# Moving the load and conversion of half of w_in from the attention stretch into the experts' stretch

## The chip, the cores and the metric

The kernel runs on one core of one Trainium2 chip. Times are device microseconds (us) of one launch. Several runs are made of each kernel, and the median is compared. One more execution is recorded by the hardware profiler; it has its own time and its own span, from its first to its last instruction.

## The reference

```
x = attention(q_l, k_l, v_l, q_g, k_g, v_g)        # 4 batches, 8 heads, 512 local + 32 global tokens, head size 64,
                                                   # local window of 32 on both sides; softmax
x = x as [2176 tokens, 512]
logits = x @ phi                                   # 512 x 32: 8 experts of 4 slots
d = softmax of logits over the tokens; slot_input = d.T @ x
for e in 8 experts: slot_out[e] = relu(slot_input[e] @ w1[e]) @ w2[e]      # w1[e] 512 x 1024, w2[e] 1024 x 512
c = softmax of logits over the slots; x = c @ slot_out
out = (relu(x @ w_in) ** 2) @ w_out                # w_in 512 x 2048, w_out 2048 x 512
```

w_in and w_out arrive as 8-byte floats; everything else is 4-byte. The kernel makes 4-byte floats of w_in and w_out itself, with integer operations.

## The kernel before, in words

The program has three stretches, and each engine runs its instructions in the order in which the code issues them.

**Attention** (0 to 182 us in the profile) is a loop over 44 units (a block of 32 queries, local or global, half of the heads). At step n of the loop (line 708) the scores of unit n are made (`emit_S`, line 314), the exponentials of unit n-1 (`emit_exp`), the transposes of unit n-2 (`emit_T`), and the products with V of two older units together (`emit_AV`, line 367; `av_at`, line 633, says at which step). V lies in a ring of three blocks (`load_v`, line 165). The block for the next pair of units can be loaded only when the products of the present pair have read the oldest block, so `load_v(s + 3)` is issued behind them (line 682), and the next products wait for it. K and Q blocks are loaded the same way, with four transfers each. All loads of this stretch, but for the first four, are issued by SyncE (SP), whose one queue the 16 DMA engines serve; a load that has to wait on SP holds up all that are behind it.

**Weights of the experts.** w1 and w2 are 64 pieces of 512 KB, loaded in the order of the list `order` (line 567) by `load_piece` (line 573). A piece needs a room, a granule of 1,024 floats on each of 128 partitions, in arena A, B or T; `room` (line 126) lists the free ones. Attention begins with 23 free rooms. The tuple `PIECES` (line 309) says how many pieces are asked for at each of the 44 steps; an ask without a room does nothing. 20 more rooms come free inside and at the end of attention (`free`, line 595: each room given is used at once), so 43 pieces are on their way when attention ends. The other 21 wait until the experts' multiplies have used up a piece and `done` (line 811) gives its room back.

**The first half of w_in** (8 chunks of 512 KB) is loaded and converted within attention. `win_load` (line 558) puts a chunk into the buffer `cv_raw` and is issued at steps 3, 7, 12, 16, 21, 25, 30 and 34; `win_convert` (line 562) gives five parts, placed on later steps by `CONV` and `CONV_AT` (line 299): `split` and mostly `rest` on ScalarE (ACT), `clamp`, `shift` and half of `join` on VectorE (DVE), the last addition on GpSimd (POOL). The result goes to `win_sb`, four granules of A that hold nothing else. `cv_raw` and the two scratch halves `cv_y` and `cv_r` take two granules of B until steps 38 and 39.

**Experts** (182 to 221 us). `layer1(gr, c0, c1)` multiplies the slots of four experts with w1 (line 902), `layer2` with w2 (line 929); the calls are in lines 956 to 989. A piece of w2 holds 128 rows of two experts, in runs of 2 KB. A room that comes free is asked for the next load at once (`fill`). Near the end of the list stands the first chunk of w_out ("raw"); 15 more chunks of w_out and the second half of w_in follow in the last stretch. After `layer2_T(1)` (line 989), `G_direct` (line 1029) multiplies the experts' output with `win_sb`.

**The final network** (221 us to the end) is bound by its multiplies (lines 1107 to 1109).

Of the kernel before, what the change touches and what calls it, by code (L numbers as in the profile page):

```python
# [10 lines left out]
I32 = mybir.dt.int32  # L11
# [13 lines left out]
def local_global_attention__soft_moe__relu2_kernel(  # L25
# [15 lines left out]
    nc = tc.nc  # L41
# [66 lines left out]
    q_buf = Bq.carve(H, 2 * D)  # L108
    cv_raw = Bq.carve(DM, 2).bitcast(I32)
    cv_y, cv_r = Bq.carve(DM), Bq.carve(DM).bitcast(I32)  # L110
    kT = Bq.carve(HP, B, 8, QB)
# [13 lines left out]
    tri = pe_buf[2][:, 0, 0:2 * QB].rearrange("p (n q) -> p n q", n=2)  # L125
    room = {"a": A.granules(7, 23), "b": Bq.granules(15, 22), "t": []}

# [141 lines left out]
    for s in range(NJ):  # L269
# [28 lines left out]

    CONV = (4, 9, 13, 18, 22, 27, 31, 36)
    CONV_AT = (  # L300
        (0, 0, 1, 2, 3), (-1, 1, 1, 2, 3), (0, 0, 1, 2, 3), (0, 0, 0, 2, 3), (0, 1, 1, 2, 3), (0, 0, 0, 2, 3),
        (0, 1, 2, 2, 3), (0, 0, 1, 1, 2),
    )
    REST_ON_ACT = (0, 0, 1, 0, 1, 1, 1, 1)

    MOE_D = (3, 4, 5)
    MOE_AT = ((0, 2, 2), (0, 1, 0), (0, 1, 2))

    PIECES = (
        0, 0, 0, 0, 1, 2, 0, 0, 1, 1, 1, 1, 0, 1, 1, 2, 0, 1, 1, 2, 0, 0, 0, 1, 1, 1, 1, 0, 1, 2, 1, 3, 0, 1,  # L310
        0, 1, 0, 0, 0, 0, 2, 2, 1, 1,
    )
# [244 lines left out]

    def win_load(n):
        c, f = divmod(n, WRES)
        convert_load(cv_raw, w_in[128 * c:128 * c + 128, 2 * CW * f:2 * CW * f + 2 * CW])  # L560

    def win_convert(n):
        c, f = divmod(n, WRES)
        return convert(cv_raw, win_sb[:, c, CW * f:CW * f + CW].bitcast(I32), cv_y, cv_r, REST_ON_ACT[n], nc.gpsimd)


    order = [(1, 4 * g + j, c) for g in range(2) for c in range(NC) for j in range(4)]
    order += [(2, 4 * g + j, c) for g in range(2) for c in range(8) for j in range(0, 4, 2)]
    order.insert(62, ("raw", 0, 0))
    piece, raws = {}, {}  # L570
    nxt = [0]

    def load_piece():
        if nxt[0] == len(order):
            return False
        kind, e, c = order[nxt[0]]
        if kind == "raw":
            if not room["a"]:
                return False
            nxt[0] += 1  # L580
            return raw_load()
        at = next((r for r in ("tba" if kind == 2 and e >= 4 else "tab") if room[r]), None)
        if at is None:
            return False
        v = g = room[at].pop(0)
        nxt[0] += 1
        if kind == 1:
            nc.sync.dma_start(out=v, in_=w1[e, 128 * c:128 * c + 128, :])
        else:
            v = v.rearrange("p (e f) -> p e f", e=2)  # L590
            nc.sync.dma_start(out=v, in_=w2[e:e + 2, 128 * c:128 * c + 128, :].rearrange("e p f -> p e f"))
        piece[kind, e, c] = (v, at, g)
        return True
# [11 lines left out]
    with tc.manual_schedule():  # L605
# [46 lines left out]
        for i in range(NM - 1):  # L652
            l1 = ("l", NT * i + NT - 1, 1)
            d = av_at(index[l1]) - index[l1]
            for fns, pos, dd in zip(((moe_logits,), (moe_TT, moe_c_exp), (moe_S,)), MOE_AT[i], MOE_D):
                for fn in fns:
                    at(l1, pos, fn, i, d=d + dd)
        for n in range(NC * WRES):
            split, clamp, shift, rest, join = win_convert(n)
            u = units[CONV[n]]  # L660
            for f, pos, d in zip((split, rest, clamp, shift, join), (2, 2, 2, 2, 0), CONV_AT[n]):
                at(u, pos, f, d=d)
            if n + 1 < NC * WRES:
                after(u, win_load, n + 1, d=CONV_AT[n][-1])
        for n in range(2):
            after(u, free, "b", 2 + n, 3 + n, d=CONV_AT[-1][-1] + n)
        after(("l", 12, 0), free, "b", 0, 1)
# [37 lines left out]
        load_vg()  # L705
        late.setdefault(3, []).append((win_load, (0,)))
        late.setdefault(5, []).insert(0, (load_phi, ()))
# [101 lines left out]
        ps_h = ctx.enter_context(tc.tile_pool(name="ps_h", bufs=2, space=PSUM))  # L809

        def done(kind, e, c):
            _, at, g = piece.pop((kind, e, c))
            room[at].append(g)


# [113 lines left out]
        def layer2(gr, c0, c1):  # L929
            for c in range(c0, c1):  # L930
                for n in range(2):
                    if c == 0:
                        hps[2 + gr, n] = ps_o.tile([128, 256], F32, tag="o", name="ops")
                    for j in range(4):
                        e = 4 * gr + j
                        nc.tensor.matmul(hps[2 + gr, n][32 * j:32 * j + 32], hT[gr][:, 16 * c + SE * j:16 * c + SE * j + 32],
                                         piece[2, e - e % 2, c][0][:, e % 2, 256 * n:256 * n + 256], start=(c == 0),
                                         stop=(c == 7))
                for j in range(0, 4, 2):
                    done(2, 4 * gr + j, c)  # L940
                fill()
                if gr and c == 6:
# [33 lines left out]
        layer2_T(0)  # L976
        assert nxt[0] == len(order)
        yro = [room["a"].pop(0) for _ in range(3)]
# [199 lines left out]
```

## Time and profile before

| | |
|---|---|
| median of 3 runs (lowest to highest) | 445.91 us (445.83 to 448.59) |
| the profiled execution's own time | 447.44 us |
| its span | 444.7 us |
| mean granted clock of TensorE | 0.983 |
| busy: PE / DVE / ACT / POOL | 403.9 / 295.9 / 230.8 / 130.4 us |
| bytes moved by DMA | 68.94 MB |

How to read it: PE is TensorE, SP the queue on which SyncE issues loads. "Idle before" is the time in which an engine did nothing ahead of an instruction, and behind the arrow stands what ended it. The granted clock is a share of 2.4 GHz; 0.50 is 1.2 GHz. A PE that is called busy may be working at the lower clock. L167 is line 167: V loads; L525: chunks of w_in and w_out; L588 and L591: pieces of w1 and w2.

### The profile page before, as it was taken

The numbers are of one execution on the slowest core, as the hardware profiler recorded it, in microseconds if no ns is written. First come the engines' busy times: TensorE is split into PE (matmuls) and PEld (weight loads), VectorE is DVE, ScalarE is ACT, GpSimd is POOL, SyncE is SP. The second block draws the span as 40 slices with busy tenths as digits, with TensorE's granted clock in tenths as the row PEclk, the third lists the DMA queues.
The fourth block names the chain that finished last, engine by engine and source line by source line (L and its number), as shares of the span: only waits on it lengthen the run. The fifth ranks groups of instructions, "written<-read, shape, count | busy, mean of one in ns | idle before, by whom it ended". The sixth has DMA issues, their size and how long they took to land.

```text
span 444.7 us, 11332 instructions
## 1 busy us (share of the span) xinstructions
PE 403.9 (91%) x4387; PEld 310.4 (70%) x4387; DVE 295.9 (67%) x956; ACT 230.8 (52%) x535; POOL 130.4 (29%) x161
## 2 busy tenths in 40 slices
PE   7898789688789868999799999999999999999996
PEld 6677667576568655346368878787887888788885
DVE  5588756476787957521289999886998454744443
ACT  3678656588456423131257666566666444344442
POOL 6234424254245423120045542224554000000000
PEclk9999989899998989999999999999999999999999
DMA  8999999789995688899963333410000300300003
GB/s 153 193 256 208 246 248 238 190 187 243 229 211 145 180 253 286 307 377 387 400 235 96 109 127 96 141 50 0 0 2 7 136 0 1 143 1 1 0 0 118
DMA packets 58212, 68.94 MB, mean 155 GB/s; under 512 B 23216, under 2 KB 39600, under 8 KB 58160
## 3 DMA queue, kind: packets, MB, share of 16 engines
q1 hardware_dynamic: 55920, 65.61, 54.2%
q10 hardware_dynamic: 2240, 2.62, 1.9%
q8 instruction: 34, 0.56, 0.5%
q14 instruction: 18, 0.15, 0.1%
HBM read 63.77 MB, written 4.46 MB: 153 GB/s over the span
## 4 chain that ended last, share of the span: by engine, by line
PE 51%; DMA 23%; DVE 14%; issue 5%; ACT 4%; SPq 1%; POOL 1%; ACTq 0%; POOLq 0%; DVEq 0%
DMA arena_b<-in_v_l_dram 13%; PE ops L1107 9%; PE ops L1108 9%; PE ops L1109 9%; PE xp L383 4%; PE sp L326 4%; PE hps L909 3%; DMA arena_a<-in_moe_w_out_dram 3%; DMA arena_b<-in_moe_w_in_dram 3%; DMA arena_b<-in_moe_w_dram 3%; DVE arena_a L535 3%; PE hp L1073 2%; DVE al L1084 2%; DVE arena_a L548 2%; PE pp L364 2%
## 5 line engine op out<-in xcount | busy, mean ns | idle before, releaser
L1107 PE MATMUL ops<-w_hl,ah 128*128 128x512 f32 x272 | 107.6, 396 | 0.0
L1108 PE MATMUL ops<-w_hl,ah 128*128 128x512 f32 x272 | 106.7, 392 | 0.4 <-POOL w_hl L851 0.4
L1109 PE MATMUL ops<-w_hl,al 128*128 128x512 f32 x272 | 106.2, 390 | 0.0
L1077 DVE TENSOR_TENSOR arena_a<-hp,arena_a 128x384 f32<-128x384 f32 x96 | 46.8, 528 | 46.8 <-ACT arena_a L1076 46.6
L1076 ACT ACTIVATE arena_a<-hp 128x384 f32<-128x384 f32 x96 | 40.2, 471 | 68.6 <-PE hp L1073 63.4
L1109 PEld LDWEIGHTS ops<-w_hl,al 128*128 128x128 f32 x272 | 51.1, 188 | 11.6 <-DVE al L1084 0.6
L1107 PEld LDWEIGHTS ops<-w_hl,ah 128*128 128x128 f32 x272 | 51.0, 188 | 11.0 <-issue 0.8
L1108 PEld LDWEIGHTS ops<-w_hl,ah 128*128 128x128 f32 x272 | 51.1, 188 | 10.5 <-POOL w_hl L851 1.8
L1083 ACT ACTIVATE ah<-arena_a 128x384 fp32r<-128x384 f32 x96 | 45.0, 505 | 24.9 <-DVE arena_a L1077 24.9
L1084 DVE TENSOR_TENSOR al<-arena_a,ah 128x384 fp32r<-128x384 f32 x96 | 49.9, 560 | 8.2 <-ACT ah L1083 4.2
L347 POOL TENSOR_TENSOR arena_r<-arena_r,nm 128x512 f32<-128x512 f32 x32 | 35.7, 1115 | 65.9 <-DVE nm L334 47.6
L139 ACT ACTIVATE arena_b<-tp 64x256 f32<-64x256 f32 (+2 forms) x131 | 42.5, 348 | 16.5 <-PE tp L216 11.4
L383 PE MATMUL xp<-arena_b,arena_t 128*32 128x65 f32 x1408 | 26.7, 224 | 20.7 <-DMA arena_b<-in_v_l_dram 17.6
L550 POOL TENSOR_TENSOR arena_a<-arena_a 128x512 int32<-128x512 int32 x23 | 29.8, 1295 | 50.7 <-DVE arena_a L548 48.2
L383 PEld LDWEIGHTS xp<-arena_b,arena_t 128*32 128x32 f32 x1408 | 22.2, 111 | 26.3 <-issue 10.0
L326 PE MATMUL sp<-arena_b 128*64 128x128 f32 x512 | 38.5, 297 | 1.5 <-ACT arena_b L139 1.5
L334 DVE CUSTOM_DVE_ANT_0 arena_r<-sp,arena_r 128x128 f32<-128x128 f32 x128 | 29.5, 286 | 14.8 <-PE sp L326 14.0
L326 PEld LDWEIGHTS sp<-arena_b 128*64 128x64 f32 x512 | 30.2, 147 | 11.2 <-issue 8.8
L356 ACT ACTIVATE arena_r<-arena_r 128x512 f32<-128x512 f32 x44 | 27.6, 627 | 11.0 <-POOL arena_r L347 10.7
L364 PE MATMUL pp<-ident,arena_r 128*128 128x128 f32 x176 | 30.2, 297 | 2.8 <-ACT arena_r L356 2.8
L851 POOL TENSOR_TENSOR w_hl<-arena_a,w_hl 128x512 fp32r<-128x512 f32 x16 | 21.4, 1336 | 33.5 <-DMA arena_a<-in_moe_w_out_dram 17.6
L364 PEld LDWEIGHTS pp<-ident,arena_r 128*128 128x128 f32 x176 | 19.5, 145 | 9.5 <-ACT arena_r L356 3.7
(181 smaller groups left out, 574.0 us busy)
## 6 DMA issues: line engine op xcount, KB each, us to landing
arena_a<-in_moe_w_dram SPq DMA_DIRECT2D x35, 512.0 KB, 9.4
arena_b<-in_moe_w_dram SPq DMA_DIRECT2D x25, 512.0 KB, 7.8
arena_a<-in_moe_w_out_dram SPq DMA_DIRECT2D x16, 512.0 KB, 7.1
arena_b<-in_v_l_dram SPq DMA_DIRECT2D x16, 256.0 KB, 5.8
arena_b<-in_moe_w_in_dram SPq DMA_DIRECT2D x8, 512.0 KB, 6.2
arena_a<-in_moe_w_in_dram SPq DMA_DIRECT2D x8, 512.0 KB, 3.9
arena_b<-in_k_l_dram SPq DMA_DIRECT2D x30, 128.0 KB, 5.7
arena_b<-in_q_l_dram SPq DMA_DIRECT2D x30, 128.0 KB, 4.9
```

Of the source, the lines that this page charges most:

```text
L139: nc.scalar.activation(out=out, in_=in_, func=AF.Copy)
L326: nc.tensor.matmul(sp[r, 2 * h + b // 2], q, keys, start=True, stop=True)
L347: nc.gpsimd.tensor_tensor(out=pe, in0=pe, in1=nm.unsqueeze(2).to_broadcast([128, 4, 128]), op=ALU.subtract)
L364: nc.tensor.transpose(pp[:, j], pe_buf[n % NPE][:, j], ident)
L383: nc.tensor.matmul(xp[32 * b:32 * b + 32, 2 * h + e], p, V[:, b, 4 * half + 2 * h + e], start=True, stop=True)
L1076: nc.scalar.activation(out=r[:, :N], in_=hp[:, :N], func=AF.Relu)
L1077: nc.vector.tensor_tensor(out=a[:, :N], in0=hp[:, :N], in1=r[:, :N], op=ALU.mult)
L1083: nc.scalar.activation(out=ah[:, s], in_=a, func=AF.Copy)
L1084: nc.vector.tensor_tensor(out=al[:, s], in0=a, in1=ah[:, s].bitcast(F32), op=ALU.subtract)
L1107: nc.tensor.matmul(op, ah[:, s], w_hi, start=begin, stop=False)
L1108: nc.tensor.matmul(op, ah[:, s], w_lo, start=False, stop=False)
L1109: nc.tensor.matmul(op, al[:, s], w_hi, start=False, stop=end)
```

## The change

- `win_sb`'s four granules and the two conversion granules of B become rooms at the start: 29 instead of 23. The first four pieces of w1 go into `win_sb`'s granules; these, and the granule of the fifth piece, are not given back (`KEPT`). The fifth one becomes the conversions' scratch.
- The eight chunks of w_in leave attention, with all their instructions. In `order` they stand among the pieces of w2: one chunk ahead of each four pieces. `layer2` converts a chunk ahead of every other c, into `win_sb`.
- `PIECES` asks for one piece more at steps 21, 27, 32, 34, 36 and 38. As the 23 or 29 rooms run out, what this gives is: the chunk at 21 is replaced by a piece; steps 25 and 30 have one load fewer; 27 has one more; 31 has three more and 32 one more; 34, 38 and 39 have one fewer each. The chunks at 3, 7, 12 and 16 are not replaced.
- A piece of w2 becomes 256 rows of one expert, two adjacent rows to a partition: runs of 4 KB instead of 2 KB. The transposes of the hidden layer read every other column to match, and `layer2` gives rooms back after every second c, four at a time.
- Counted out, 47 loads (32 of w1, 12 of w2, 3 chunks of w_in) are on their way when attention ends, instead of 43 pieces and 8 chunks. 25 loads and the first chunk of w_out are left for the experts' stretch, instead of 21 and that chunk. The list's last two pieces still stand behind the chunk of w_out.

```
-    cv_raw = Bq.carve(DM, 2).bitcast(I32)
-    cv_y, cv_r = Bq.carve(DM), Bq.carve(DM).bitcast(I32)
+    Bq.carve(2 * GR)
...
-    room = {"a": A.granules(7, 23), "b": Bq.granules(15, 22), "t": []}
+    room = {"a": A.granules(0, 4) + A.granules(7, 23), "b": Bq.granules(2, 4) + Bq.granules(15, 22), "t": []}
...
-    CONV = (4, 9, 13, 18, 22, 27, 31, 36)
...
-        0, 0, 0, 0, 1, 2, 0, 0, 1, 1, 1, 1, 0, 1, 1, 2, 0, 1, 1, 2, 0, 0, 0, 1, 1, 1, 1, 0, 1, 2, 1, 3, 0, 1,
-        0, 1, 0, 0, 0, 0, 2, 2, 1, 1,
+        0, 0, 0, 0, 1, 2, 0, 0, 1, 1, 1, 1, 0, 1, 1, 2, 0, 1, 1, 2, 0, 1, 0, 1, 1, 1, 1, 1, 1, 2, 1, 3, 1, 1,
+        1, 1, 1, 0, 1, 0, 2, 2, 1, 1,
...
-    order += [(2, 4 * g + j, c) for g in range(2) for c in range(8) for j in range(0, 4, 2)]
-    order.insert(62, ("raw", 0, 0))
+    for n in range(2 * NC):
+        order += [("win", n, 0)] + [(2, 4 * (n // NC) + j, n % NC) for j in range(4)]
+    order.insert(70, ("raw", 0, 0))
+    KEPT = [(1, j, 0) for j in range(4)] + [(1, 0, 1)]
...
+        if kind == "win":
+            at = next((r for r in "tba" if room[r]), None)
...
+            g = room[at].pop(0)
+            f, c = divmod(e, NC)
+            convert_load(g.rearrange("p (n w) -> p n w", w=2).bitcast(I32),
+                         w_in[128 * c:128 * c + 128, 2 * CW * f:2 * CW * f + 2 * CW])
...
-            v = v.rearrange("p (e f) -> p e f", e=2)
-            nc.sync.dma_start(out=v, in_=w2[e:e + 2, 128 * c:128 * c + 128, :].rearrange("e p f -> p e f"))
+            v = v.rearrange("p (r f) -> p r f", r=2)
+            nc.sync.dma_start(out=v, in_=w2[e, 256 * c:256 * c + 256, :].rearrange("(p r) f -> p r f", r=2))
...
-        for n in range(NC * WRES):
-            split, clamp, shift, rest, join = win_convert(n)
...
-            if n + 1 < NC * WRES:
-                after(u, win_load, n + 1, d=CONV_AT[n][-1])
-        for n in range(2):
-            after(u, free, "b", 2 + n, 3 + n, d=CONV_AT[-1][-1] + n)
...
+        def win_convert(n):
+            at, g = wins.pop(n)
+            f, c = divmod(n, NC)
+            y = kept[-1][1]
+            split, clamp, shift, rest, join = convert(
+                g.rearrange("p (n w) -> p n w", w=2).bitcast(I32), win_sb[:, c, CW * f:CW * f + CW].bitcast(I32),
+                y[:, 0:CW], y[:, CW:].bitcast(I32), True, nc.gpsimd)
+            for fn in (split, rest, clamp, shift, join):
+                fn()
+            room[at].append(g)
+            fill()
...
-                    nc.tensor.transpose(tp[:, c], tmp[:, 128 * (4 * n + c):128 * (4 * n + c) + 128], ident)
+                    f0 = 512 * n + 256 * (c // 2) + c % 2
+                    nc.tensor.transpose(tp[:, c], tmp[:, f0:f0 + 255:2], ident)
...
         def layer2(gr, c0, c1):
             for c in range(c0, c1):
+                if c % 2 == 0:
+                    win_convert(NC * gr + c // 2)
...
-                                         piece[2, e - e % 2, c][0][:, e % 2, 256 * n:256 * n + 256], start=(c == 0),
+                                         piece[2, e, c // 2][0][:, c % 2, 256 * n:256 * n + 256], start=(c == 0),
...
-                for j in range(0, 4, 2):
-                    done(2, 4 * gr + j, c)
-                fill()
+                if c % 2:
+                    for j in range(4):
+                        done(2, 4 * gr + j, c // 2)
+                    fill()
```

## Rows read from the trace of the kernel before

**Rows 1.** The page's 40 slices of 11.1 us: busy tenths of PE and DMA.
```profile
PE   7898789688789868999799999999999999999996
...
DMA  8999999789995688899963333410000300300003
```

**Rows 2.** Chain that ended last, attention: start us, duration, what.
```profile
20.04 7.63 DMA arena_b<-in_moe_w_in_dram
...
44.28 7.19 DMA arena_b<-in_v_l_dram
...
74.85 8.42 DMA arena_b<-in_v_l_dram
...
105.12 8.36 DMA arena_b<-in_v_l_dram
...
154.91 7.44 DMA arena_b<-in_v_l_dram
```

**Rows 3.** Who waited for whom: us in total, times, longest us.
```profile
PE xp L383 <- DMA arena_b<-in_v_l_dram: 17.6, 10, 4.0
ACT arena_b L532 <- DMA arena_b<-in_moe_w_in_dram: 12.5, 4, 6.0
```

**Rows 4.** PE over time: start, us, instruction [idle before <-what ended it].
```profile
60.60 0.37 PE L216 MATMUL tp<-ident,arena_b 128*128 128x128 f32 x1 [2.15 <-issue]
...
83.31 0.91 PE L383 MATMUL xp<-arena_b,arena_t 128*32 128x65 f32 x48 [3.62 <-DMA arena_b<-in_v_l_dram]
...
132.04 0.92 PE L364 MATMUL pp<-ident,arena_r 128*128 128x128 f32 x4 [1.80 <-ACT arena_r L356]
...
135.65 0.96 PE L383 MATMUL xp<-arena_b,arena_t 128*32 128x65 f32 x52
...
162.48 0.81 PE L383 MATMUL xp<-arena_b,arena_t 128*32 128x65 f32 x37 [3.96 <-DMA arena_b<-in_v_l_dram]
```

**Rows 5.** Stretches: busy us of PE, PEld, DVE, ACT, POOL; clock; DMA.
```profile
60.60:64.00 3.40, 3.40 (x23) 2.77 (x23) 0.93 (x8) 3.22 (x10) 0.00 (x0) 0.50 1.25 200
84.50:87.90 3.40, 3.40 (x24) 2.95 (x24) 1.74 (x4) 1.55 (x8) 0.00 (x0) 0.50 0.22 73
...
213.00:220.50 7.50, 4.92 (x47) 1.45 (x37) 2.63 (x5) 1.22 (x2) 0.00 (x0) 1.00 1.04 403
```

**Rows 6.** PE around the experts, in order of time.
```profile
181.99 7.07 PE L909 MATMUL hps<-arena_a,slots 128*32 128x512 f32 x64 [0.38 <-DVE slots L793]
...
204.71 4.50 PE L936 MATMUL ops<-arena_a,c_all 128*32 128x256 f32 x80
...
219.44 0.41 PE L936 MATMUL ops<-arena_t,c_all 128*32 128x256 f32 x2 [0.72 <-DMA arena_t<-in_moe_w_dram]
```

**Rows 7.** Stretches as in rows 5; last three columns: clock, DMA share, GB/s.
```profile
182.00:213.00 31.00, 31.00 (x385) 14.75 (x389) 6.38 (x23) 5.79 (x12) 3.30 (x12) 1.00 0.97 355
...
183.30:185.30 2.00, 2.00 (x24) 0.65 (x20) 1.57 (x5) 0.00 (x0) 0.64 (x2) 1.00 0.22 41
...
190.00:200.00 10.00, 10.00 (x100) 4.29 (x96) 2.35 (x9) 3.11 (x6) 2.28 (x8) 1.00 1.04 384
219.40:224.40 5.00, 4.45 (x85) 3.19 (x85) 3.28 (x8) 2.10 (x4) 1.30 (x1) 1.00 1.02 409
27.70:83.30 55.60, 43.62 (x915) 35.21 (x914) 38.02 (x198) 38.49 (x99) 23.24 (x23) 0.97 1.10 241
```

**Rows 8.** Issue and landing of the pieces issued at 183.9 and 207.0 us.
```profile
L591 SPq DMA_DIRECT2D arena_a<-in_moe_w_dram x1: 368/368/368, 183.9 to 183.9; - x1
...
DMA to landing us min/median/max: 3.4/3.4/3.4
...
L591 SPq DMA_DIRECT2D arena_t<-in_moe_w_dram x1: 368/368/368, 207.0 to 207.0; - x1
...
DMA to landing us min/median/max: 12.4/12.4/12.4
```

**Rows 9.** The page's group of the conversions' last part: busy us, mean ns.
```profile
L550 POOL TENSOR_TENSOR arena_a<-arena_a 128x512 int32<-128x512 int32 x23 | 29.8, 1295 | 50.7 <-DVE arena_a L548 48.2
```

More of the change, by code (lines that the diff above doesn't have):

```diff
@@ L297, in local_global_attention__soft_moe__relu2_kernel @@
     X_AT = (2, 2, 2, 2, 2, 0, 2, 2, 2, 0, 0, 2, 2, 1, 1, 2)
-    CONV = (4, 9, 13, 18, 22, 27, 31, 36)
[L300 to L304, printed above, removed]
     MOE_D = (3, 4, 5)
@@ L556, in local_global_attention__soft_moe__relu2_kernel @@
     WRES = NCW // 2
[L558 to L564, printed above, removed]
-    order = [(1, 4 * g + j, c) for g in range(2) for c in range(NC) for j in range(4)]
-    order += [(2, 4 * g + j, c) for g in range(2) for c in range(8) for j in range(0, 4, 2)]
-    order.insert(62, ("raw", 0, 0))
+    order = [(1, 4 * g + j, c) for g in range(2) for c in range(NC) for j in range(4)]
+    for n in range(2 * NC):
+        order += [("win", n, 0)] + [(2, 4 * (n // NC) + j, n % NC) for j in range(4)]
+    order.insert(70, ("raw", 0, 0))
+    KEPT = [(1, j, 0) for j in range(4)] + [(1, 0, 1)]
+    wins = {}
     piece, raws = {}, {}
@@ L581, in load_piece @@
             return raw_load()
+        if kind == "win":
+            at = next((r for r in "tba" if room[r]), None)
+            if at is None:
+                return False
+            nxt[0] += 1
+            g = room[at].pop(0)
+            f, c = divmod(e, NC)
+            convert_load(g.rearrange("p (n w) -> p n w", w=2).bitcast(I32),
+                         w_in[128 * c:128 * c + 128, 2 * CW * f:2 * CW * f + 2 * CW])
+            wins[e] = (at, g)
+            return True
         at = next((r for r in ("tba" if kind == 2 and e >= 4 else "tab") if room[r]), None)
@@ L657, in local_global_attention__soft_moe__relu2_kernel @@
                     at(l1, pos, fn, i, d=d + dd)
-        for n in range(NC * WRES):
-            split, clamp, shift, rest, join = win_convert(n)
-            u = units[CONV[n]]
-            for f, pos, d in zip((split, rest, clamp, shift, join), (2, 2, 2, 2, 0), CONV_AT[n]):
-                at(u, pos, f, d=d)
-            if n + 1 < NC * WRES:
-                after(u, win_load, n + 1, d=CONV_AT[n][-1])
-        for n in range(2):
-            after(u, free, "b", 2 + n, 3 + n, d=CONV_AT[-1][-1] + n)
         after(("l", 12, 0), free, "b", 0, 1)
@@ L705, in local_global_attention__soft_moe__relu2_kernel @@
         load_vg()
-        late.setdefault(3, []).append((win_load, (0,)))
         late.setdefault(5, []).insert(0, (load_phi, ()))
@@ L809, in local_global_attention__soft_moe__relu2_kernel @@
         ps_h = ctx.enter_context(tc.tile_pool(name="ps_h", bufs=2, space=PSUM))
+        kept = []
         def done(kind, e, c):
             _, at, g = piece.pop((kind, e, c))
+            if (kind, e, c) in KEPT:
+                kept.append((at, g))
+            else:
+                room[at].append(g)
[8 more added lines that the diff above has]
+                fn()
             room[at].append(g)
+            fill()
         seq = [("o", m) for m in range(8)] + [("i", k) for k in range(2 * NC)] + [("o", m) for m in range(8, NFC)]
@@ L976, in local_global_attention__soft_moe__relu2_kernel @@
         layer2_T(0)
-        assert nxt[0] == len(order)
+        assert nxt[0] == len(order) and kept[-1][0] == "a"
         yro = [room["a"].pop(0) for _ in range(3)]
```

## The prediction

> **What bounds the kernel now.** I first read the page's slices [rows 1]. PE is the engine nearest to full, but its digits fall in attention, and there the DMA row stands at 8 and 9 up to 135 us and again until 220 us. So there are two stretches to look at, attention and the experts, and in both the suspect is the load queue. Behind the experts nothing is changed.
>
> In attention the chain of waits [rows 2] says which loads matter: it runs through V transfers, 7 to 8 us from issue to landing where they are longest, and the first chunk of w_in stands on it itself. The totals of waits [rows 3] say what that costs: PE stood 17.6 us for V, ten times, and ACT 12.5 us for chunks of w_in, four times. PE in order of time [rows 4] shows where: 3.62 us ahead of 83.31, 3.96 ahead of 162.48. Two idle times have another cause. Ahead of 60.60 and 132.04 ACT sat in front of a `split` whose chunk had not landed, and what stood behind it on ACT was late. After each of these four idle times PE ran 3.4 us at clock 0.50, the 1.2 GHz level (two of the four are in [rows 5]). A fully busy stretch of 3.4 us at that level holds 1.7 us of full-clock work, so each costs up to 1.7 us more.
>
> At the experts PE starts at 181.99 [rows 6] and is busy throughout to 213, while DMA carries 355 GB/s [rows 7]. Then it waits: the last piece lands at 207.0 + 12.4 = 219.4 [rows 8], and PE begins on it at 219.44 [rows 6]. So the end of this stretch is the end of its loads. They can't start earlier: from 183.3 to 185.3 DMA moves 41 GB/s [rows 7], because every room is full until the first pieces of w1 are used up.
>
> **The change, part by part.** One load of 512 KB is 0.524 MB: 1.28 us at the 409 GB/s of the stretch with 4 KB runs alone (w_out and w_in), 1.37 at the 384 GB/s of the 2 KB runs, and 2.18 at the 241 GB/s of early attention, where short K, Q and V rows are mixed in [rows 7].
>
> Attention, in order of time:
> - The chunks at steps 3, 7, 12 and 16 go with no replacement. DMA is saturated from 27.7 to 83.3 (share 1.10), so what is taken out of the queue comes back as time at the V landing that ends at 83.3 [rows 2]. Bounds: 4 x 1.28 = 5.1 and 4 x 2.18 = 8.7. I take 1.4 each, 5.6, near the lower end, since the mixed rate is slow through rows that stay. ACT's waits and PE's 2.15 us at 60.60 lie inside this stretch and are not counted again: V is what is late next.
> - One load fewer in front of the V transfer of 105.12: 1.28 to 2.18, I take 1.3.
> - The slow stretch at 84.5 [rows 5] goes only if the idle time ahead of it shrinks enough: 0 to 1.7, I take 0.5.
> - Around 132 the blocked ACT goes, 1.80 us, and perhaps the slow stretch behind it, 1.7. But step 31 now asks for three more pieces, ahead of the V load that step 32 issues: four loads replace a chunk and a piece there. Two more loads are 2.6 us, and PE takes up that V block at 135.65 [rows 4]. Between a loss of 2.6 (PE waits for both) and a gain of 3.5 (both hidden); I take a loss of 0.5, as this V load becomes what is late.
> - Two loads fewer stand in front of the V transfer of 154.91: 2.6, at most the 3.96 of idle [rows 4]; I take 2.7. The slow stretch behind it: 0 to 1.7, I take 0.6.
>
> Sum: 5.6 + 1.3 + 0.5 - 0.5 + 2.7 + 0.6 = **10.2 us shorter**. The lower ends give 6.4. The upper ends give 21.8; I stop at 15, as the idle times for V are 17.6 in all and PE must find everything else ready.
>
> The experts, from the start of their multiplies:
> - The first four pieces' rooms don't come back, so the first load waits for the second quarter of the 7.07 us [rows 6]: 1.8 us later, with nothing else for DMA to do.
> - 26 loads instead of 22. With 4 KB runs 26 x 1.28 = 33.3 against 22 x 1.37 = 30.1: 3.2. From the first landing, 183.9 + 3.4 = 187.3, to the last, 219.4, the other 21 took 1.53 each [rows 8], interruptions included; 4 x 1.53 = 6.1 is the upper end. I take 3.6.
> - The last piece now holds rows for two values of c. By the code 26 multiply instructions and an idle product stand behind it, instead of 12. At 4.50 us for 80 [rows 6] that is 0.8; 0.9 with the idle product.
> - PE keeps clock 1.00 in its last waits, with 4.92 of 7.5 us busy [rows 5]. Now a chunk and four pieces, 6.4 us of loads, bring it 32 instructions, 1.8 us of work. I add one slow stretch, 1.7; bounds 0 and 3.4.
>
> Sum: 1.8 + 3.6 + 0.9 + 1.7 = **8.0 us longer**; ends 5.9 and 12.2.
>
> The row on which the second of these terms rests is that of 4 KB runs, 409 against 384 GB/s [rows 7]. The Trainium skill, "DMA: Bandwidth & Descriptors" (Specifications), asks for 512 bytes or more for full line rate, which runs of 2 KB and of 4 KB both have. By that rule the longer runs bring nothing, the 26 loads cost 2.3 us more, and the whole sum would come out at no change. The trace speaks against it a little, though not on the same data.
>
> **What costs nothing.** The conversions go one after another through one scratch. POOL's part takes 1.3 us [rows 9]; with ACT's and DVE's ahead of it I take twice that from one chunk to the next, ten us for the first four. Cover: DVE, ACT and POOL are busy 3 to 6 of 31 us there [rows 7], and PE doesn't read `win_sb` before the end. If the cover is gone: the first chunk of w_out takes the room of chunk 3, and the last two pieces stand behind it on SP. A load is issued up to 12.4 us ahead of its landing [rows 8]; chunk 3 done by 209 leaves about that. What else it could cost is a piece or two late, 1.3 to 2.6. The transposes that read every other column are 16 instructions in a stretch that waits for DMA.
>
> **Sum.** 10.2 - 8.0 = 2.2 us faster. The profiled execution took 447.44 us with a span of 444.7, 1.5 over the median of the runs. From its time the sum gives 445.2, and from the median, which I forecast, **443.7**.
>
> **The rivals.**
> - *The relief comes through in full* (0.26). PE loses most of its idle time for V and all four slow stretches, 14.5 us; the experts pay 6.5. 445.9 - 8 = 438. For: each idle time shortened brings the next V load forward. Against: PE is already 78% busy between them (43.62 of 55.60 [rows 7]).
> - *V waits on its own traffic* (0.14, slower). The V transfers of 44.28 and 154.91 were about as long as any (7.19 and 7.44 [rows 2]) with no chunk of w_in just ahead. If the short rows of K, Q and V, not the 512 KB loads, set V's landing, attention gains only 2.5, while the experts still pay 8: 451.4. It decides at the landing now at 83.3: if that comes less than 3 us sooner, this is the case. Against: a DMA share of 1.10 means that whatever is removed shortens the queue.
> - *TensorE goes slow at the end of the experts* (0.12). Between the late pieces PE falls to 0.50 and stays there into `G_direct` and the first multiplies of the final network: two slow stretches more than I counted, 443.7 + 3.4 = 447.1. For: idle times of 1.8 to 4 us came ahead of all four slow stretches [rows 4, 5]. Against: nothing slow follows the waits of 213 to 220.5 (clock 1.00), and idle products stand in this stretch. The Trainium skill, "TensorE: Matmul & The Clock Gate" (Loop structure matters more than you think), warns of just this loop, a long DMA wait between multiplies, and says that the engine then runs cold; the slow rows agree.
> - The forecast itself, with its own range of 441 to 446.5, has 0.48.
>
> **Chances.** Over 1% is 4.5 us, about what a measurement of this kernel tells from no change. Faster: 0.24 from the first rival and 0.07 from the forecast's edge, 0.31. Slower: 0.12 from the second and 0.02 from the third, 0.14. Within 1%: 0.55. The ends of the terms are 15 - 5.9 = 9.1 faster and 12.2 - 6.4 = 5.8 slower, 436.8 to 451.7; I give 437 to 450.5.
>
> **What would show it.** Right: no wait of ACT for w_in in attention; experts that start near 172 instead of 181.99; a first load there issued 1.8 us later after that start than now; and 43 us from that start to the last piece's landing instead of 37.4. Wrong: a start of the experts after 178 (second rival) or before 169 (first); a stretch to the last piece no longer than now, if the queue had slack; waits on chunks of w_in that hold up the last pieces, if the conversions are not covered; a V wait near 125 longer than the loss that I took.

## The result, and the profile after

The changed kernel is a little slower: 450.39 us at the median of 16 runs (447.56 to 460.81), against 446.24 for the kernel before (16 runs, 442.26 to 448.59). The ratio is 1.0104, 95% interval 1.0071 to 1.0137. A second comparison gave 450.56 (4 runs) and 1.0134, interval 1.0072 to 1.0197. The forecast of 443.7 lay on the other side of no change.

The first recorded execution of the changed kernel (458.68 us) was a disturbed one, so all rows of it here come from a second recording (451.41 us, span 448.8, mean granted clock 0.977), and the ratios here and below leave such runs out, while medians and ranges hold all runs.

The page's slices of PE and DMA, to be held against [rows 1]:

```profile
PE   7899697988848988997699999999999999999996
...
DMA  8979989899783588799943333230000300300003
```

In the twelfth slice (123 to 135 us) PE falls to 4, a hole that the kernel before didn't have. The chain of waits shows what is in it (start us, duration, what):

```profile
73.11 5.56 DMA arena_b<-in_v_l_dram
...
98.74 7.06 DMA arena_b<-in_v_l_dram
...
121.12 10.02 DMA arena_b<-in_v_l_dram
...
152.48 5.93 DMA arena_b<-in_v_l_dram
```

Beside [rows 2] the chunk of w_in is gone from the chain and three V transfers are shorter. (Another on the chain, issued at 64.00, is longer: 7.87 us, where the one of 66.62 in the kernel before took 6.38.) But a V transfer that had not been among the long ones now takes 10.02 us, more than any before. The totals of waits (us in total, times, longest us):

```profile
PE xp L376 <- DMA arena_b<-in_v_l_dram: 16.8, 7, 6.1
...
PE ops L946 <- DMA arena_a<-in_moe_w_dram: 1.9, 1, 1.9
```

PE's wait for V is 16.8 us instead of 17.6 [rows 3]: nearly the same total, but 6.1 of it in one place. ACT has no wait for w_in left. PE in order of time, with the idle time ahead of each:

```profile
105.84 0.85 PE L376 MATMUL xp<-arena_b,arena_t 128*32 128x65 f32 x44 [1.51 <-DMA arena_b<-in_v_l_dram]
...
131.27 1.96 PE L376 MATMUL xp<-arena_b,arena_t 128*32 128x65 f32 x64 [6.10 <-DMA arena_b<-in_v_l_dram]
...
158.54 1.14 PE L376 MATMUL xp<-arena_b,arena_t 128*32 128x65 f32 x64 [2.44 <-DMA arena_b<-in_v_l_dram]
...
177.62 4.93 PE L916 MATMUL hps<-arena_a,slots 128*32 128x512 f32 x44 [0.38 <-DVE slots L783]
...
218.91 0.64 PE L946 MATMUL ops<-arena_t,c_all 128*32 128x256 f32 x1 [0.46 <-DMA arena_t<-in_moe_w_dram]
...
220.75 2.08 PE L265 MATMUL idle<-c_all,ident 128*128 128x512 f32 x2
...
232.18 0.50 PE L1118 MATMUL ops<-w_hl,ah 128*128 128x512 f32 x1
```

The experts start at 177.62, 4.4 us earlier than at 181.99 [rows 6], where 10.2 had been forecast; the multiply on the last piece is at 218.91, and the final network starts at 232.18. Stretches of the same kernel (columns as in [rows 5, 7], the last three are clock, DMA share and GB/s):

```profile
129.10:135.90 6.80, 4.63 (x100) 3.93 (x100) 2.22 (x7) 0.00 (x0) 0.00 (x0) 0.50 0.60 171
159.90:163.30 3.40, 3.40 (x41) 2.65 (x40) 1.56 (x11) 1.21 (x3) 0.00 (x0) 0.50 0.78 283
...
190.00:200.00 10.00, 10.00 (x125) 5.15 (x126) 4.64 (x11) 5.37 (x11) 2.70 (x5) 1.00 1.01 402
213.00:217.90 4.90, 1.67 (x7) 0.41 (x6) 2.80 (x5) 2.25 (x4) 1.81 (x2) 1.00 1.03 410
217.90:224.70 6.80, 6.34 (x31) 1.74 (x29) 3.27 (x7) 0.77 (x2) 1.26 (x1) 0.50 1.03 410
```

Two stretches at 1.2 GHz are 6.8 us long, where all four of the kernel before were 3.4. In the first of them PE still stands idle until 131.27 and is busy for 4.63 us. The second covers the work behind the last piece. The loads of three places, by line and time of issue:

```profile
L588 SPq DMA_DIRECT2D arena_b<-in_moe_w_dram x4: 430/453/739, 118.8 to 120.5; - x4
...
DMA to landing us min/median/max: 5.1/6.6/9.4
...
L518 SPq DMA_DIRECT2D arena_a<-in_moe_w_in_dram x1: 328/328/328, 181.3 to 181.3; - x1
...
L591 SPq DMA_DIRECT2D arena_t<-in_moe_w_dram x1: 328/328/328, 208.7 to 208.7; - x1
...
DMA to landing us min/median/max: 10.2/10.2/10.2
```

Four pieces are issued in the 2.4 us ahead of the V load of 121.12. The first load of the experts is issued at 181.3, 3.7 after their start. The last piece lands at 208.7 + 10.2 = 218.9.

### The profile page after: what moved, and what is told of

The parts are those of the page before. It is cut to its first block, busy times and chain, and to the rows that moved or that the text cites. A ratio compares the mean times of both kernels' runs of the same rounds, so it can differ in the third digit from the quotient of the medians.

```text
span 455.6 us, 11350 instructions
## 1 busy us (share of the span) xinstructions
PE 414.0 (91%) x4387; PEld 313.9 (69%) x4387; DVE 299.9 (66%) x953; ACT 233.5 (51%) x538; POOL 127.4 (28%) x161
## 4 chain that ended last, share of the span: by engine, by line
PE 52%; DMA 21%; DVE 14%; ACT 6%; issue 5%; POOL 1%; ACTq 0%; POOLq 0%; DVEq 0%; SPq 0%
DMA arena_b<-in_v_l_dram 11%; PE ops L1118 9%; PE ops L1119 9%; PE ops L1120 9%; PE xp L376 6%; PE sp L319 4%; PE pp L357 4%; DVE arena_a L528 3%; ACT arena_b L139 3%; DVE al L1095 3%; DMA arena_a<-in_moe_w_dram 2%; DMA arena_b<-in_moe_w_dram 2%; DMA arena_t<-in_moe_w_dram 2%; PE hp L1084 2%; PE hps L916 2%
## 5 line engine op out<-in xcount | busy, mean ns | idle before, releaser
L543 POOL TENSOR_TENSOR arena_a<-arena_a 128x512 int32<-128x512 int32 x31 | 39.9, 1287 | 67.6 <-DVE arena_a L541 62.7
L340 POOL TENSOR_TENSOR arena_r<-arena_r,nm 128x512 f32<-128x512 f32 x32 | 33.3, 1040 | 69.2 <-DVE nm L327 49.5
L376 PE MATMUL xp<-arena_b,arena_t 128*32 128x65 f32 x1408 | 28.9, 235 | 21.0 <-DMA arena_b<-in_v_l_dram 13.2
L376 PEld LDWEIGHTS xp<-arena_b,arena_t 128*32 128x32 f32 x1408 | 24.1, 118 | 26.3 <-issue 9.7
L349 ACT ACTIVATE arena_r<-arena_r 128x512 f32<-128x512 f32 x44 | 27.6, 628 | 17.9 <-POOL arena_r L340 17.6
L357 PE MATMUL pp<-ident,arena_r 128*128 128x128 f32 x176 | 31.3, 305 | 0.7 <-ACT arena_r L349 0.7
L139 ACT ACTIVATE arena_t<-pp 128x512 f32<-128x512 f32 x27 | 16.1, 597 | 27.5 <-PE pp L357 27.3
L528 DVE TENSOR_SCALAR arena_a<-arena_a 128x512 f32<-128x512 f32 x32 | 24.6, 768 | 6.4 <-ACT arena_a L525 6.4
```

Of the source, the lines that this page charges most:

```text
L139: nc.scalar.activation(out=out, in_=in_, func=AF.Copy)
L357: nc.tensor.transpose(pp[:, j], pe_buf[n % NPE][:, j], ident)
L376: nc.tensor.matmul(xp[32 * b:32 * b + 32, 2 * h + e], p, V[:, b, 4 * half + 2 * h + e], start=True, stop=True)
L543: add.tensor_tensor(out=dst, in0=dst, in1=r, op=ALU.add)
```

## Where the time went

Between the two recordings the span grew by 448.8 - 444.7 = 4.1 us:

| us | before | after | difference | forecast |
|---|---|---|---|---|
| attention, to the first multiply of the experts | 181.99 | 177.62 | -4.4 | -10.2 |
| experts: start to first load | 1.9 | 3.7 | +1.8 | +1.8 |
| first load to last piece's landing | 35.5 | 37.6 | +2.1 | +3.6 |
| that landing to the first multiply of the final network | 8.7 | 13.3 | +4.6 | +2.6 |
| final network | 216.6 | 216.6 | 0 | 0 |

(The final network began at 228.1 in the kernel before.) The experts cost 8.5, close to the forecast's 8.0. Attention gained 5.8 less than forecast, and that is the sign of the result.

## The experiments

The theory was that attention loses most of its gain at the V transfer of 121.12 because step 31 issues three more pieces ahead of it, and the rest of the loss stands behind the last piece. The rivals are named in each expectation.

**no_win**: the kernel before without the loads and the conversions of this half of w_in; the half is zero in it.

```
-            for f, pos, d in zip((split, rest, clamp, shift, join), (2, 2, 2, 2, 0), CONV_AT[n]):
-                at(u, pos, f, d=d)
-            if n + 1 < NC * WRES:
-                after(u, win_load, n + 1, d=CONV_AT[n][-1])
...
+        nc.gpsimd.memset(win_sb.rearrange("p c f -> p (c f)"), 0.0)
```

> The kernel before without w_in's first half: its eight loads and eight conversions in attention are left out (zeros are written to win_sb instead, so this half of w_in is missing from the result). Nothing takes their place. Queue theory: attention was bound by the load queue in front of V, so it ends 8 to 10 us before 182, and the whole is 437 to 439. Rival (PE's own order and its slow-clock stretches set attention, the queue only fills the gaps): attention ends at 179 or later, and the whole is 443 or more.

438.62 us (4 runs), ratio to the kernel before 0.9866, interval 0.9802 to 0.9929: in the theory's range. PE in time:

```profile
175.81 1.08 PE L903 MATMUL hps<-arena_a,slots 128*32 128x512 f32 x4 [0.38 <-DVE slots L786]
```

The experts start 6.2 us earlier than in the kernel before (181.99), not the theory's 8 to 10, and the ratio is worth 6.0. The edit takes some of its own gain away, just ahead of the experts, where GpSimd writes the zeros. In no_win (by engine, then time):

```profile
168.57 3.96 DVE L768 TENSOR_SCALAR arena_r<-blk,w 32x32 f32<-32x32 f32 x2
168.98 3.52 POOL L788 MEMSET arena_a<- 128x4096 f32 x1
...
168.85 0.40 PE L762 MATMUL mtp<-arena_r 32*128 32x32 f32 x2
173.19 0.73 PE L777 MATMUL sip<-s_run,arena_r 128*32 128x128 f32 x6 [3.29 <-DVE s_run L520]
```

The same VectorE instructions and the same multiplies (L762 above) in the kernel before:

```profile
178.78 0.51 DVE L775 TENSOR_SCALAR arena_r<-blk,w 32x32 f32<-32x32 f32 x2
...
179.07 0.40 PE L769 MATMUL mtp<-arena_r 32*128 32x32 f32 x2
```

At these multiplies no_win is 10.2 us ahead (168.85 against 179.07). Then two VectorE instructions that took 0.51 us take 3.96 and end with the writing of the zeros, PE waits 3.29 us for what follows them, and it runs at 1.2 GHz from 171.3 to 181.5. So the half costs about 10 us in attention, by the queue as the theory had it, and 6.2 is what this edit left of it. There was something to gain by moving the half.

**late31**: the kernel after without the pieces of step 31. The asks of later steps, which found no room in the changed kernel, take them up one by one; when attention ends the same number of loads is on its way.

```
-        0, 0, 0, 0, 1, 2, 0, 0, 1, 1, 1, 1, 0, 1, 1, 2, 0, 1, 1, 2, 0, 1, 0, 1, 1, 1, 1, 1, 1, 2, 1, 3, 1, 1,
+        0, 0, 0, 0, 1, 2, 0, 0, 1, 1, 1, 1, 0, 1, 1, 2, 0, 1, 1, 2, 0, 1, 0, 1, 1, 1, 1, 1, 1, 2, 1, 0, 1, 1,
```

> The changed kernel with step 31 asking for no piece instead of three; the later asks of one each take them up, behind the V load of step 32. Queue theory: the gain of some 5.7 us that attention has at 108 us was taken back by these three pieces in front of the V load of step 32 (4.6 us of PE idle). That wait falls to 2 us or less, attention ends 3 to 5 us earlier than in the changed kernel, and the whole is 445 to 447.5. Rival (the gain goes to PE's own order and slow clock whatever stands in the queue): within 1 us of the changed kernel, 449.5 to 451.

445.23 us (10 runs), ratio to before 0.9973, interval 0.9925 to 1.0021: 5.2 below the kernel after, for one digit, and the intervals of the two ratios don't meet (1.0071 to 1.0137 there). PE in time:

```profile
127.75 0.45 PE L376 MATMUL xp<-arena_b,arena_t 128*32 128x65 f32 x17 [2.15 <-DMA arena_b<-in_v_l_dram]
...
172.85 0.64 PE L916 MATMUL hps<-arena_a,slots 128*32 128x512 f32 x4 [0.38 <-DVE slots L783]
```

and its chain:

```profile
121.54 6.07 DMA arena_b<-in_v_l_dram
```

The V transfer issued at 121.54 takes 6.07 instead of 10.02, PE waits 2.15 instead of 6.10, and the experts start at 172.85, where the forecast had put them ("near 172"). So the three pieces took attention's gain, shown by taking them away. The recordings of the other runs agree. With the three pieces ahead of that V load (the kernel after, kept_last and tail_after) PE waits 4.4 to 7.1 us and the experts start at 177.6 to 177.9. Without them (late31, both, warm, three and three2) it waits 1.5 to 2.8 us and they start at 169.4 to 173.0. That the kernel becomes faster than the one before isn't shown by this edit alone: the interval of its ratio includes 1.

**v_first**: the same three pieces, asked for one step later, behind that V load.

```
-        0, 0, 0, 0, 1, 2, 0, 0, 1, 1, 1, 1, 0, 1, 1, 2, 0, 1, 1, 2, 0, 1, 0, 1, 1, 1, 1, 1, 1, 2, 1, 3, 1, 1,
+        0, 0, 0, 0, 1, 2, 0, 0, 1, 1, 1, 1, 0, 1, 1, 2, 0, 1, 1, 2, 0, 1, 0, 1, 1, 1, 1, 1, 1, 2, 1, 0, 4, 1,
```

> Kernel after, with the three extra pieces of w1 of step 31 asked for in step 32, behind its V load instead of ahead of it; the same loads in number and size. If position is what counts (theory): the V load issued near 122 lands some 6 us after its issue instead of 8.5, PE waits about 2 us for it instead of 4.6, the experts start near 173 to 175, and the time is 445 to 447. If the sheer amount of 512 KB loads counts (rival), the same wait comes back at the next V block, near 140, the experts start at 177 to 178 as with the three pieces ahead, and the time stays at 449 to 451.

448.53 us (4 runs), ratio 1.0112, interval 1.0026 to 1.0199: half a us under the rival's bound and 1.5 over the theory's. The traces decide, and the theory of position fell. Its chain and then PE in time:

```profile
123.22 4.55 DMA arena_b<-in_v_l_dram
...
129.10 8.21 DMA arena_b<-in_v_l_dram
```

```profile
137.44 0.86 PE L376 MATMUL xp<-arena_b,arena_t 128*32 128x65 f32 x22 [4.13 <-DMA arena_b<-in_v_l_dram]
...
177.58 0.64 PE L916 MATMUL hps<-arena_a,slots 128*32 128x512 f32 x4 [0.38 <-DVE slots L783]
```

The V load of 123.22 lands fast, but five pieces issued from 123.6 to 126.5 now stand ahead of the next one, issued at 129.10: it takes 8.21, PE waits 4.13, and the experts start at 177.58, within 0.1 of the changed kernel. In these two kernels what counts is how many 512 KB loads stand between two V loads, whichever V load comes next. In this stretch V loads follow each other by about 6 us. As an estimate, four pieces at 1.28 and the V block itself, half their size, fill that alone (5.8), and four Q transfers come on top; late31 puts one or three into such an interval and spreads the others over later ones.

**kept_last**: the kernel after with its rooms in another order, so that the four pieces kept in `win_sb` are not the first ones used.

```
-    room = {"a": A.granules(0, 4) + A.granules(7, 23), "b": Bq.granules(2, 4) + Bq.granules(15, 22), "t": []}
+    room = {"a": A.granules(7, 23) + A.granules(0, 4), "b": Bq.granules(2, 4) + Bq.granules(15, 22), "t": []}
-    KEPT = [(1, j, 0) for j in range(4)] + [(1, 0, 1)]
+    KEPT = [(1, 3, 3)] + [(1, 4 + j, 0) for j in range(4)]
```

> The changed kernel with win_sb's granules given to the pieces that the second group uses first, so that the first four rooms come back at once as in the kernel before. Theory (late restart of the loads costs 1.8 us and more at a slow clock): the first load of the experts is issued 1.9 us after their first multiply instead of 3.6 to 5.2, and the whole is 1.8 to 3.3 us less than the changed kernel, 447 to 448.6. Rival (the load queue has slack in this stretch): no change, 450 to 451.

451.89 us (4 runs from 448.5 to 456.85), ratio 1.0136, interval 1.0059 to 1.0214: no gain in time, with an interval too wide for 1.7 us. In its trace the first load is issued 1.94 us after the experts' first multiply, and PE begins on the last piece 40.0 us after it (217.94 against 177.92) instead of 41.3: a gain of 1.3 in the stretch.

**both**: late31 and kept_last together.

> Kernel after, without the three pieces at step 31 and with the kept rooms moved so that the first four pieces of w1 give theirs back at once. Theory: the two gains add, the first load of the experts is issued 1.9 us after their first multiply instead of 3.7, and the time is 443 to 444.5, about 1.7 below that of the kernel without the three pieces alone (445.2). Rival: the queue's start is hidden by what comes at the end (products at 1.2 GHz behind the last piece), and the time is 445 to 446.

443.81 us (10 runs), ratio 0.9931, interval 0.9878 to 0.9984. Its first load of the experts:

```profile
L518 SPq DMA_DIRECT2D arena_a<-in_moe_w_in_dram x1: 328/328/328, 172.1 to 172.1; - x1
```

with the experts' first multiply at 170.21, 1.9 ahead of it. The median is 1.4 below late31, near the theory's 1.7, but the two intervals overlap. The late restart is shown in the traces and only made likely in the times.

**runs4k**: the kernel before with the pieces of w2 in runs of 4 KB and nothing else.

```
-            v = v.rearrange("p (e f) -> p e f", e=2)
-            nc.sync.dma_start(out=v, in_=w2[e:e + 2, 128 * c:128 * c + 128, :].rearrange("e p f -> p e f"))
+            v = v.rearrange("p (r f) -> p r f", r=2)
+            nc.sync.dma_start(out=v, in_=w2[e, 256 * c:256 * c + 256, :].rearrange("(p r) f -> p r f", r=2))
```

> The kernel before with only the 4 KB runs of w2 (256 rows of one expert in a piece, every other column in the transposes). By the trace of the kernel before: 22 loads at 1.28 instead of 1.37 us are 2.0 us less, the coarser last pieces cost 0.9, so 445, about 1 us less than the kernel before. By a rule that both run lengths are at full rate: 0.9 us slower, 447.

447.79 us at the median of 10 runs from 438.61 to 452.51, above the kernel before beside it (445.23), but a ratio of 0.992, interval 0.9864 to 0.9976, below it. In time it is undecided. The rate can be read from its trace, in a stretch of w2 pieces:

```profile
196.00:206.00 10.00, 10.00 (x120) 4.77 (x116) 1.98 (x8) 2.80 (x6) 1.93 (x8) 1.00 1.02 409
```

409 GB/s, against 384 for runs of 2 KB [rows 7]. 512 KB at these rates are 1.28 and 1.37 us. The Trainium skill, "DMA: Bandwidth & Descriptors" (Specifications), puts both above the 512 bytes it asks for; by that the rates would be equal, and the measurement decides otherwise.

**warm** and **three**: late31, and both, with another end of the second layer: idle products in the waits, and the last two values of c multiplied expert by expert.

```
+            for j in range(4):
+                idle_products(1, ps_h, "h", c_flat[:, :512 if j == 0 else 256])
+                for c in range(6, 8):
+                    for n in range(2):
+                        nc.tensor.matmul(hps[3, n][32 * j:32 * j + 32], hT[1][:, 16 * c + SE * j:16 * c + SE * j + 32],
+                                         piece[2, e, 3][0][:, c % 2, 256 * n:256 * n + 256], start=False,
+                                         stop=(c == 7))
```

> Kernel after, without the three pieces at step 31 and with the end of the experts' second layer written otherwise: idle products fill the waits for the last pieces, one behind the last pieces is taken out, and the last pair of c is multiplied expert by expert, so that a quarter of the work stands behind the last piece. Theory: TensorE stays at 2.4 GHz there, from the last landing to the first multiply of the final network it takes 9 to 10 us instead of 13.3, and the time is 441.5 to 442.5. Rival: the clock falls all the same, or the work behind the last piece was never the wait, and the time is 445 to 446.

> All three edits together (no three pieces at step 31, rooms given back at once, end of the second layer with the idle products in its waits). Theory: the gains add, 439.5 to 441, below both the kernel before and the kernel after. Rival: one of them takes the place of another, and the time is 442 or more.

444.60 us (10 runs, ratio 0.998, interval 0.9924 to 1.0035) and 445.40 (10 runs, 1.0011, 0.9963 to 1.0059): nothing gained on late31 and on both. Both theories failed; three lies where its rival had it, and warm 0.4 below its rival's range. PE of three:

```profile
204.21 1.93 PE L946 MATMUL ops<-arena_b,c_all 128*32 128x256 f32 x32
...
207.13 1.91 PE L964 MATMUL ops<-arena_b,c_all 128*32 128x256 f32 x8
...
214.55 1.91 PE L964 MATMUL ops<-arena_t,c_all 128*32 128x256 f32 x8
```

32 instructions of four experts took 1.93; 8 of one expert took 1.91. The four experts write to four groups of 32 output partitions and run side by side; one after another they take four times as long (4 x 1.91 = 7.6). The edit gained the clock (1.00 from 200 to 224 us) and lost the gain again by the order.

**after_again**: the kernel after once more, for the rows above.

> The changed kernel as it stands, beside the kernels below on the same chip. Expected by every theory: 448 to 451.5. Its trace should show the experts starting near 177 to 178, a V wait of PE of more than 4 us near 133, the first load of the experts 3.5 to 5.5 us after their first multiply, and 11 to 14 us from the last landing to the first multiply of the final network.

450.56 us (4 runs). All four marks were met: 177.62, a V wait of 6.10, 3.7 and 13.3 us.

**tail_after**: the kernel after with the idle products in the waits and the multiplies in their old order.

```
-                if gr and c == 6:
-                    idle_products(1, ps_h, "h", c_flat[:, :512])
+                if gr and c in (4, 6):
+                    idle_products(2 if c == 4 else 1, ps_h, "h", c_flat[:, :512])
...
+                        if gr and c == 6 and n == 0 and j:
+                            idle_products(1, ps_h, "h", c_flat[:, :256])
```

> Kernel after with the idle product behind c = 6 taken away and idle products put ahead of c = 4 and c = 6 and between the first multiplies of c = 6, all where TensorE waits for pieces; the multiplies keep their order. Theory: TensorE is at 2.4 GHz when the last piece lands, from that landing to the first multiply of the final network it takes 9 to 10 us instead of 11.5 to 13.3, and the time is 446.5 to 448.5, some 2.5 to 3.5 below the kernel after. Rival: the length of this stretch is the work and the evictions behind it, not the clock; the stretch stays above 11.5 us and the time at 449 to 451.5.

449.07 us (10 runs, 444.07 to 451.3), ratio 1.0069, interval 1.0026 to 1.0112. Its stretches ahead of the last piece and behind it, and PE:

```profile
213.00:217.90 4.90, 3.81 (x16) 1.30 (x12) 2.81 (x5) 2.23 (x4) 1.84 (x2) 1.00 1.03 410
217.90:224.70 6.80, 6.44 (x102) 3.87 (x100) 5.66 (x12) 2.88 (x6) 2.52 (x2) 1.00 1.03 409
```

```profile
218.93 0.40 PE L950 MATMUL ops<-arena_t,c_all 128*32 128x256 f32 x1
...
228.80 0.50 PE L1120 MATMUL ops<-w_hl,ah 128*128 128x512 f32 x1
```

From 218.9 to 228.8 are 9.9 us instead of 13.3, at clock 1.00: as the theory had it, 3.4 us less in the trace. Not all of that is the clock, since the edit also takes away an idle product that stood behind the last piece, 2.08 us at 220.75 in the kernel after. The kernel before has the same product ahead of its last piece, at clock 1.00:

```profile
216.44 1.13 PE L265 MATMUL idle<-c_all,ident 128*128 128x512 f32 x2
```

So, as an estimate, 1.1 of the 3.4 is this product and 2.3 the clock; no run parts the two. At this place the clock falls to 0.50, for 3.4 to 6.8 us, in every recording of a changed kernel without the fillers (the kernel after, late31, both, kept_last, v_first), and in none with them (tail_after, warm, three, three2, thin).

The medians differ by 1.5, and their intervals overlap; 449.07 falls short of the expected 446.5 to 448.5 and lies at the lower end of the rival's range, while the trace is as the theory had it. The Trainium skill, "TensorE: Matmul & The Clock Gate" (Loop structure matters more than you think), says that multiplies between long DMA waits run cold; the rows of both kernels agree (0.50 without the fillers, 1.00 with them), though the longest wait here is 1.93 us.

**three2**: late31, kept_last and tail_after together.

> Three edits of the kernel after: no three pieces at step 31, the first rooms given back at once, and the idle products in the waits of the last pieces (multiplies in the old order, four experts side by side). Theory: the three losses were separate and are all gone, 439.5 to 441.5, faster than both kernels. Rival: the end of the experts is not shortened by it, 443 to 445, as without the idle products.

441.90 us (12 runs, 437.33 to 447.1), ratio to before 0.9917, interval 0.9876 to 0.9958. It beats the kernel before and the kernel after; 0.4 above what the theory gave, and below the rival's 443. PE at the V block of late31:

```profile
125.98 0.73 PE L376 MATMUL xp<-arena_b,arena_t 128*32 128x65 f32 x37 [1.61 <-DMA arena_b<-in_v_l_dram]
```

Here no stretch at 1.2 GHz follows the wait (clock 1.00 from 125.9 to 139.2), and the experts start at 169.41.

**thin**: three2 with one piece moved from step 29 to step 37 (the expectation calls it 38).

```
-        0, 0, 0, 0, 1, 2, 0, 0, 1, 1, 1, 1, 0, 1, 1, 2, 0, 1, 1, 2, 0, 1, 0, 1, 1, 1, 1, 1, 1, 2, 1, 0, 1, 1,
-        1, 1, 1, 0, 1, 0, 2, 2, 1, 1,
+        0, 0, 0, 0, 1, 2, 0, 0, 1, 1, 1, 1, 0, 1, 1, 2, 0, 1, 1, 2, 0, 1, 0, 1, 1, 1, 1, 1, 1, 1, 1, 0, 1, 1,
+        1, 1, 1, 1, 1, 0, 2, 2, 1, 1,
```

> As the kernel with the three edits, and one of the two pieces of step 29, which stands ahead of the V load issued near 121, is asked for at step 38 instead, where DMA is a third to a half full. Theory (what stands ahead of a V load costs its transfer time if PE waits there): the wait near 127 falls from about 2 us by up to 1.3, and the time is 0.5 to 1.5 below that kernel, 438.5 to 440.5. Rival: the piece then stands ahead of the V load issued near 146 to 148, whose wait of 2 us grows by as much, and nothing is gained.

439.79 us (6 runs, 436.83 to 445.73), ratio 0.9898, interval 0.9841 to 0.9956. Its recording took 437.48, with stretches and PE as follows:

```profile
168.90:219.10 50.20, 47.47 (x542) 22.31 (x542) 31.14 (x64) 22.26 (x40) 16.66 (x23) 1.00 0.98 383
```

```profile
125.24 0.96 PE L376 MATMUL xp<-arena_b,arena_t 128*32 128x65 f32 x53 [2.00 <-DMA arena_b<-in_v_l_dram]
...
168.88 1.49 PE L916 MATMUL hps<-arena_a,slots 128*32 128x512 f32 x12 [0.38 <-DVE slots L783]
...
219.09 0.50 PE L1120 MATMUL ops<-w_hl,ah 128*128 128x512 f32 x1
```

This is the fastest kernel here that computes the whole result, though not told apart from three2, whose interval overlaps. The wait that the edit was to shorten is 2.00 at 125.24, against 1.61 in three2, so the step's reason is not borne out. The expectation had the place wrong: in three2 the pieces of step 29 are issued by 107.4, ahead of the V load of 114.45, on whose block PE doesn't wait, and not of the one of 120.31. What thin has over three2 in its recording it has ahead of that place (PE takes up a V block at 104.47 instead of 105.84). Beside the kernel before, the experts start 13.1 us earlier, and the stretch of 50.2 from there to the final network, wholly at clock 1.00, is 4.1 longer.

## Why the prediction was wrong

By its own steps, with V transfers as marks (the lead is how much earlier the changed kernel comes to a mark than the kernel before):

- *The chunks at steps 3, 7, 12 and 16, the V of 105.12 and the slow stretch at 84.5* (5.6 + 1.3 + 0.5 = 7.4). The V block that landed at 105.12 + 8.36 = 113.5 [rows 2] landed at 105.8: 7.7. The sum is right, by parts that made up for each other: the first was 4.6 (the landing of 83.3 is at 78.7) instead of 5.6, the V transfer is 1.3 shorter as taken, and the slow stretch went altogether, up to 1.7 instead of 0.5. One reading isn't shown: that ACT caused the 2.15 us ahead of 60.60. Its row names issue, not ACT, and the changed kernel, with no chunk of w_in there, still has waits that end so, 0.55 us ahead of 59.46 and 1.46 ahead of 114.43. The sum didn't count it.
- ***Around 132* (a loss of 0.5, at worst 2.6). This is the step that failed.** Up to the issue of the next long V transfer (154.91 before, 152.48 after) the lead falls from 7.7 to 2.4: a loss of 5.3. The step named the cause, three more pieces ahead of the V load of step 32, and priced the two extra loads at 2.6, near the mark: that V block landed 7.1 us after its issue in the kernel before (128.08) and 10.0 now (121.12). Of the 5.3, 0.7 is gone by that issue. PE takes up the block 4.4 earlier (131.27 against 135.65 [rows 4]), so 2.6 goes there, the whole of the step's worst case. Another 2.1 goes by the V load issued at 146.54 (148.88 before), where the lead is 2.3. The step failed in three ways. It took ACT's relief of 1.8 and the vanished slow stretch of 1.7 as a credit against the late V, when a wait for a later V swallows both: PE arrives earlier and stands idle until the V block lands. It let the slow stretch vanish or stay where it was, ahead of the V block; now it lies behind the landing, where PE is busy in it for 4.63 us, which is up to 2.3 lost, about the 2.1 above. (three2, with no slow stretch there, has a lead of 9.7 at that block and still 9.7 at its V load of 139.19, the one of 148.88 before.) And it put the chosen value at 0.5, near the hopeful end. late31 shows the term's size: without the three pieces the experts start at 172.85, 4.8 earlier, and the time is 5.2 less. There the lead falls by only 0.5, from 7.0 (that V block lands at 106.5) to 6.5 (the last long V load is issued at 148.4): the value that the step had taken, with the pieces gone.
- *Two loads fewer ahead of the V of 154.91* (2.7 + 0.6). The lead grew by 2.0, from 2.4 to 4.4: the idle time fell from 3.96 to 2.44, and a slow stretch of 3.4 stayed (159.9).
- *The late restart* (1.8). Right: 3.7 against 1.9, and back to 1.9 once the first rooms are given back (both).
- *26 loads instead of 22* (3.6). 2.1 in the recording, below the lower bound of 3.2. At 1.28 and 1.37 each, 26 and 22 loads would be 33.3 and 30.1; what lies above these is 4.3 now and 5.4 before, so the interruptions were shorter. The lower bound had them alike for both.
- *The coarser last piece and one slow stretch* (0.9 + 1.7). 4.6: tail_after, at clock 1.00, leaves 9.9 - 8.7 = 1.2 for the work. The other 3.4 is, by the estimate above, 1.1 for the idle product and 2.3 for the clock. So the idle product was priced at 0.1 where its like took 1.13 in the kernel before, and the clock at 1.7, between bounds that hold what it cost. The third rival's mechanism was here only in part: the lower clock ended at 224.7, ahead of `G_direct`.
- *Conversions hidden at no cost.* Right: no wait for a chunk of w_in, before or behind the experts' start.

The marks that the prediction had set read so: no wait of ACT for w_in (met), experts near 172 (177.62, just short of the 178 of the second rival), first load 1.8 later (met), 43 us to the last landing (41.2), and as a sign of failure "a V wait near 125 longer than the loss that I took": 6.10, the one that came true. The second rival gave 451.4, the closest figure, for another reason: it was decided at the landing of 83.3, which came 4.6 us sooner, more than its limit of 3. The recording of before stood 1.2 over its median of 16 runs (446.24) and that of after 1.0 over its own, so the medians parted by 4.15, as the spans did (4.1).

Not settled: why interruptions of the experts' loads are shorter after the change; and the times of single edits of 1 to 2 us, since runs of one kernel spread over 3 us and more, 14 in runs4k.

## What to carry to other kernels

Work taken out of one stretch of a saturated load queue gives time back only if what moves up to fill its place is still spread between the small loads that the compute waits for: count the big loads between two such loads, in each interval, not over the stretch. A lead gained earlier doesn't pay for a late load, because the engine only arrives sooner and waits longer; price the new wait in full, and add the clock that the engine loses in it. Where TensorE waits for loads, fill its idle time with products that nobody needs, and keep none of them behind the last load (3.4 us less in the trace of tail_after, in the times only likely); don't take apart multiplies that run side by side.

## What the runs showed of the hardware that had not been expected

- Stretches at 1.2 GHz lasted 3.4, 6.8 or 10.2 us (171.3 to 181.5 in no_win), and the idle time just ahead of one doesn't tell its length: in the kernel after, none followed 1.51 us idle at 105.84, 6.8 us went with the 6.10 idle at 131.27, and again 6.8 followed a stretch of short waits in which PE was busy for 1.67 of 4.90 us. With the fillers it was busy there for 3.81 and stayed at 2.4 GHz.
- A load of 512 KB takes 1.28 us of the queue in runs of 4 KB and 1.37 in runs of 2 KB, from the same tensor (409 GB/s in runs4k, 384 in the kernel before).
- Four groups of 32 output partitions multiplied side by side take the time of one: 1.93 us for 32 instructions of four experts, 1.91 for 8 of one.
- Two small VectorE instructions that took 0.51 us in the kernel before took 3.96 in no_win and ended with GpSimd's writing of 128x4096 zeros (3.52 us). The rows show that they end together, not why.
